# The first weight transfers of a linear-attention and MoE kernel, begun by GpSimd's DMA queue instead of SyncE's

## The chip, the cores and the metric

The kernel runs on one core of one Trainium2 chip. A core has TensorE (PE; its weight loads are listed as PEld), VectorE (DVE), ScalarE (ACT), GpSimd (POOL) and SyncE (SP), which work through queues of their own and meet by semaphores. Transfers run on 16 DMA engines and are begun by an instruction in the queue of SyncE, GpSimd or another engine. The metric is the device time of one execution in microseconds (us), the median of several runs.

## The reference

Three blocks follow each other. The first is a recurrence over 768 steps for 4 x 8 heads with a state of 40 x 40 each; the second and third are dense layers over its 3072 outputs of 320 numbers.

```python
for t in range(S):                      # B, H, S, D = 4, 8, 768, 40
    y[:, :, t] = einsum('bhd,bhde->bhe', rt, state)
    Sa = einsum('bhde,bhe->bhd', state, at)
    state = state * wt[:, :, None, :] - einsum('bhd,bhe->bhde', Sa, bt)
    state = state + einsum('bhd,bhe->bhde', vt, kt)
x = y.transpose(0, 2, 1, 3).reshape(3072, 320)
a, b = x @ w1, x @ w2                   # 320 x 1024 each
x = (a * b @ w3) @ w_out                # 1024 x 1024, 1024 x 320
h = maximum(x @ w_in, 0.0)              # 320 x 2048
return (h * h) @ w_out2                 # 2048 x 320
```

The weights come as 64-bit floats, the other inputs as 32-bit.

## The kernel before

**The scan.** The recurrence is cut into 24 chunks of 32 steps. What of a chunk doesn't depend on the state is prepared ahead (`prep`): its image `im` (k, b, a and the decay w, one transfer of 839 KB for the first chunks, in two pieces later) is loaded, VectorE makes running products of the decay (L553 `suf`, L563 `wi`), five multiplies scale the image (L575 with `wi`, L581 four times with `suf`; VectorE does them for chunks 0 to 3, GpSimd after that), TensorE multiplies the pieces (`prep_pq`, L594), ScalarE copies one half of the result (L598), VectorE transposes the other (L599 `qt`) and it is masked (L601, VectorE or GpSimd). `prep_kb` turns the scaled image (L611, ScalarE's copy L615). The results go to memory (`AW_d`, `Q_d`, `KB_d`) and are loaded again by the chunk that needs them. For four chunks at a time VectorE solves a triangular system (`solve`, from L646 to L665). It needs `pq` of all four.

**The chunk itself** is a chain through the state: `do_x0` (L739), `do_sa` (L749, copied by ScalarE to SA in L751), `do_sat` (L756, copies L758 and L761), `do_l` (L769, VectorE's L774), `do_z` and `do_ys` (L797, then VectorE's L805 and L809). `corner` (L687, L690, ScalarE's L694 and L698) finishes a piece of the first solve. Chunk c is computed while chunk c + 6 is prepared.

**The dense layers.** `w3` and `w_out` are multiplied into one matrix first (`fold`), and TensorE's gaps in the scan are filled with that and with the tiles of the second block (`a_tile`: L370 `ab`, L428 `px`) as the scan's outputs come. From 740 us on only the third block runs (L370 `ph`, L994 `po`).

**The weights.** `fetch` brings a piece of a weight matrix and decodes the 64-bit floats: a transfer (L319), two instructions of ScalarE (L325, L326) and two of VectorE (L328, L330). For `w1` and `w2` ScalarE and GpSimd then split it into two parts (L340 and L341, L353 and L354). `early` is true for `wo` (eight transfers of 320 KB), `w3t` (16 of 512 KB) and `w1` and `w2` (12 of 512 and 256 KB), and is set to false behind the scan's loop (L944), before `win` and `wo2`. The first pieces go into memory that is used later for other things (tile `early`), the rest through three buffers `raw` (`WB = (3, 4, 2)`), so such a transfer waits for the decode of the one three before.

**What sets the order.** TensorE's order is written by hand (`OPENING`, `BETWEEN`, the gaps `GAP0` and so on, and the queue `fill` of work that fills gaps). The other engines are ordered by a scheduler with priorities (`FIRST` for the chain, `SECOND` for `prep` and `solve`) that goes by estimates of when each instruction is ready. The loads and stores of `prep` go through `q_["prep"]`, which is SyncE's queue for chunks 0 to 9 and GpSimd's from chunk 10 on.

Of the kernel before, what the change touches and what calls it, by code (L numbers as in the profile page):

```python
# [243 lines left out]
def body(tc, img, rv, rd, vn, vp, raw, w1, w2, w3t, wo, win, wo2, ident, maskt, out, dbg=None):  # L244
    nc = tc.nc
    mm = nc.tensor.matmul
    act, dve, pool, sp = nc.scalar, nc.vector, nc.gpsimd, nc.sync

    with (
# [12 lines left out]
        with right, tc.manual_schedule(engines={mybir.EngineType.PE}):  # L262
# [8 lines left out]
            def staged(pl, tags, words):  # L271

                slots, n = staging.setdefault(tags, (deque(), [0]))
                if not slots:
                    t = pl.tile([128, 2048], U32, name="early", tag=tags[n[0] % len(tags)])
                    n[0] += 1
                    slots.extend(t[:, i:i + words] for i in range(0, 2049 - words, words))
                return slots.popleft()

            staging = {}  # L280
            early = True
# [13 lines left out]
            def fetch(pl, K, N, parts, dst=None, tag="fold"):  # L295

                place = None
                if early:
                    count[tag] += 1
                    if tag == "split" and count[tag] <= SPLIT_STAGED:  # L300
                        place = staged(ma, ("gh", "gl"), 1024)
                    elif tag == "fold" and not w12 and count[tag] <= FOLD_STAGED:
                        place = staged(wa, ("w1h", "w1l", "w2h"), 640)
                tag = "split" if early and tag == "split" else "wst"
                if dst is not None:
                    o = dst
                else:
                    o = pl.tile([128, K, N], F32, name="wst", tag=tag, bufs=bufs[tag])
                if not is64:
                    for p, f, src in parts:  # L310
                        sp.dma_start(out=o[p, f], in_=src)
                    return o
                if place is not None:
                    rt = place[:, 0:2 * K * N]
                else:
                    rt = pl.tile([128, 2 * K * N], U32, name="raw", tag="raw", bufs=bufs["raw"])
                rv_ = rt.rearrange("p (k n) -> p k n", k=K)
                for p, f, src in parts:
                    sp.dma_start(out=rv_[p, f], in_=src)  # L319
                w2_ = rt.rearrange("p (k n j) -> p k n j", k=K, j=2)  # L320
                hi, lo = w2_[:, :, :, 1], w2_[:, :, :, 0]
                ou = o.bitcast(U32)


                act.activation(out=o, in_=hi.bitcast(F32), func=AF.Copy, scale=2.0 ** -112)  # L325
                act.activation(out=lo, in_=lo, func=AF.Copy, scale=2.0 ** -29, bias=LOW)  # L326
                with tc.issue_after(hold[-1]) if hold else nullcontext():
                    dve.scalar_tensor_tensor(out=ou, in0=ou, scalar=3, in1=lo, op0=ALU.logical_shift_left,  # L328
                                             op1=ALU.bitwise_or)
                    dve.scalar_tensor_tensor(out=ou, in0=hi, scalar=0x80000000, in1=ou, op0=ALU.bitwise_and,  # L330
                                             op1=ALU.bitwise_or)
                return o

            def split_w(pl, src, h, l, j, k):

                n = 512 if early else 256

                t = fetch(pl, 1, n, [(slice(0, 128), 0, wcols(src, n * j, n)[128 * k:128 * k + 128])], tag="split")
                f = slice(n * j, n * j + n)
                act.copy(out=h[:, k, f], in_=t[:, 0])  # L340
                pool.tensor_tensor(out=l[:, k, f], in0=t[:, 0], in1=h[:, k, f], op=ALU.subtract)  # L341

            def split_r(pl, two):

                n = 512 if early else 256


                t = fetch(pl, 1, n, [(slice(64 * i, 64 * i + 64), 0, wcols(src, c, n)[256:320])
                                       for i, (src, c, _) in enumerate(two)], tag="split")
                for i, (_, c, r) in enumerate(two):  # L350
                    p, q = slice(64 * i, 64 * i + 64), slice(64 - 64 * i, 128 - 64 * i)
                    f = slice(c, c + n)
                    act.copy(out=r[p, f], in_=t[p, 0])  # L353
                    pool.tensor_tensor(out=r[q, f], in0=t[p, 0], in1=r[p, f], op=ALU.subtract)  # L354
# [88 lines left out]
            def fold(solved):  # L443
# [5 lines left out]
                def load_w3(i):  # L449
                    f, g = i // 2, i % 2  # L450
                    w3[i] = fetch(wf, 4, 128, [(slice(0, 128), slice(0, 4), wcols(w3t, 128 * f, 128)[
                        512 * g:512 * g + 512, :].rearrange("(k p) f -> p k f", p=128))])
# [39 lines left out]
            with (  # L492
# [381 lines left out]
                for c in range(NCH):  # L874
                    last = c == NCH - 1
                    p = c + 6
# [67 lines left out]
            early = False  # L944
# [189 lines left out]
```

## Time and profile before

| | us |
|---|---|
| median of three runs | 1076.19 |
| the three runs | 1075.29, 1082.97, 1076.19 |
| the profiled execution, its time | 1078.62 |
| the profiled execution, its span | 1076.7 |
| TensorE busy in the span | 917.4 (85%) |
| VectorE busy | 714.0 (66%) |
| ScalarE busy | 442.1 (41%) |
| GpSimd busy | 233.3 (22%) |

The span is the stretch from the first to the last instruction that the profiler recorded; the time of the execution is 1.9 us longer. Busy times of different engines overlap. Rows of a timeline give the start, the busy time, the engine (SPq is SyncE's queue of issues) and the line, then the operation, what it writes and from what, and how many such instructions are taken together. In square brackets stands how long the engine was idle just before, and what released it.

### The profile page before, as it was taken

How to read it: one execution, taken by the hardware profiler on the slowest of the kernel's cores; microseconds unless marked ns; L12 is line 12 of the kernel's file. 1: busy time of each engine (PE TensorE's matmuls, PEld its weight loads, DVE VectorE, ACT ScalarE, POOL GpSimd, SP SyncE). 2: the span in 40 equal slices, each digit the busy share in tenths (PEclk: the TensorE clock that was granted, in tenths of full speed). 3: DMA queues.
4: the chain of work that ended last, by engine and by line, in shares of the span. 5: the costliest groups of instructions: out<-in, count | busy, mean ns of one | idle time of the engine just before them, and what ended most of it. 6: DMA issues, size and time to landing. Idle time of an engine off the chain costs nothing.

```text
span 1076.7 us, 29204 instructions
## 1 busy us (share of the span) xinstructions
PE 917.4 (85%) x12240; PEld 823.3 (76%) x12240; DVE 714.0 (66%) x1399; ACT 442.1 (41%) x942; POOL 233.3 (22%) x304
## 2 busy tenths in 40 slices
PE   1327866689989898988999989879999999999997
PEld 1315544588888888887899879868989889898886
DVE  6864879958975996798589344897455554444432
ACT  2424555343434323433343333785433333333332
POOL 0261224433343343434200000562000000000000
PEclk9999988899999899989999999999999999999999
DMA  8976775666666567765744542666122221000001
GB/s 211 312 228 181 215 238 152 163 177 161 168 158 166 147 154 170 173 152 146 182 119 110 129 97 63 159 182 126 30 61 49 63 48 25 2 25 1 18 8 27
DMA packets 208922, 134.44 MB, mean 125 GB/s; under 512 B 143742, under 2 KB 184063, under 8 KB 208369
## 3 DMA queue, kind: packets, MB, share of 16 engines
q1 hardware_dynamic: 201424, 110.61, 40.3%
q0 software_dynamic: 7072, 21.57, 7.2%
q8 instruction: 98, 1.61, 0.7%
q10 hardware_dynamic: 288, 0.33, 0.1%
q14 instruction: 40, 0.32, 0.1%
HBM read 99.27 MB, written 33.19 MB: 123 GB/s over the span
## 4 chain that ended last, share of the span: by engine, by line
PE 52%; DVE 23%; DMA 12%; issue 4%; ACT 4%; SPq 2%; POOL 2%; ACTq 0%; DVEq 0%; POOLq 0%
PE ph L370 15%; PE po L994 15%; PE ab L370 9%; PE px L428 4%; DVE tmp L653 4%; DVE T L656 4%; PE pat L797 2%; DVE wst L328 2%; DVE yst L809 2%; DVE RX L805 2%; DMA im<-img 2%; DMA raw<-w3t 2%; PE pat L769 2%; DMA AW_d<-wi 2%; PE pat L782 1%
## 5 line engine op out<-in xcount | busy, mean ns | idle before, releaser
L994 PE MATMUL po<-wuh,rl 128*128 128x320 f32 x384 | 117.2, 308 | 1.7 <-DVE rl L981 1.7
L994 PE MATMUL po<-wul,rh 128*128 128x320 f32 x384 | 118.3, 308 | 0.0
L994 PE MATMUL po<-wuh,rh 128*128 128x320 f32 x384 | 118.0, 308 | 0.0
L370 PE MATMUL ab<-xh,w1h 128*128 128x256 f32 x192 | 60.0, 313 | 24.6 <-DVE g L402 23.8
L407 ACT CAST gh<-g 128x256 fp32r<-128x256 f32 x96 | 38.9, 405 | 99.2 <-DVE g L402 99.1
L370 PE MATMUL ph<-xh,wih 128*128 128x512 f32 x192 | 76.0, 396 | 2.8 <-issue 2.8
L370 PE MATMUL ph<-xh,wil 128*128 128x512 f32 x192 | 75.7, 394 | 0.0
L370 PE MATMUL ph<-xl,wih 128*128 128x512 f32 x192 | 75.6, 394 | 0.0
L994 PEld LDWEIGHTS po<-wul,rh 128*128 128x128 f32 x384 | 72.0, 188 | 4.3
L994 PEld LDWEIGHTS po<-wuh,rh 128*128 128x128 f32 x384 | 72.0, 188 | 3.8
L994 PEld LDWEIGHTS po<-wuh,rl 128*128 128x128 f32 x384 | 71.7, 188 | 2.4 <-DVE rl L981 2.2
L428 PE MATMUL px<-wph,gh 128*128 128x320 f32 x192 | 65.6, 342 | 2.7 <-ACT gh L407 2.7
L656 DVE TENSOR_TENSOR T<-T,tmp 128x31 f32<-128x31 f32 (+20 forms) x170 | 65.6, 386 | 3.0
L797 PE MATMUL pat<-YI,YR 128*40 128x72 f32 (+1 forms) x1536 | 57.4, 237 | 11.5 <-ACT kn L615 6.7
L653 DVE TENSOR_TENSOR tmp<-PT,T 128x31 f32<-128x31 f32 (+20 forms) x170 | 64.9, 382 | 3.5
L408 DVE TENSOR_TENSOR gl<-g,gh 128x256 fp32r<-128x256 f32 x96 | 45.1, 470 | 33.1 <-ACT gh L407 32.9
L581 POOL TENSOR_TENSOR im<-im,suf 104x256 f32<-104x256 f32 x80 | 65.6, 849 | 0.0
L797 PEld LDWEIGHTS pat<-YI,YR 128*40 128x40 f32 x1536 | 53.1, 125 | 16.1 <-ACT kn L615 7.3
L428 PE MATMUL px<-wph,gl 128*128 128x320 f32 x192 | 61.3, 319 | 0.8 <-DVE gl L408 0.7
L428 PE MATMUL px<-wpl,gh 128*128 128x320 f32 x192 | 60.9, 317 | 0.0
L370 PE MATMUL ph<-xq,wir 128*128 128x512 f32 x192 | 60.3, 394 | 0.0
L401 ACT COPY a_sb<-ab 128x256 f32<-128x256 f32 x96 | 35.6, 371 | 58.6 <-PE ab L370 58.1
(539 smaller groups left out, 2452.6 us busy)
## 6 DMA issues: line engine op xcount, KB each, us to landing
raw<-w3t SPq DMA_DIRECT2D x16, 512.0 KB
YR<-KB_d SPq DMA_DIRECT2D x48, 160.0 KB
im<-img POOLq DMA_DIRECT2D x28, 240.0 KB, 4.6
wt<-AW_d SPq DMA_DIRECT2D x24, 214.5 KB
raw<-wo SPq DMA_DIRECT2D x16, 320.0 KB
RX<-vp SPq DMA_DIRECT2D x24, 208.0 KB
vs<-rv SPq DMA_DIRECT2D x24, 208.0 KB
KB_d<-kn POOLq DMA_DIRECT2D x14, 320.0 KB, 5.6
```

The costliest lines, as they stand in the source:

```text
L328: dve.scalar_tensor_tensor(out=ou, in0=ou, scalar=3, in1=lo, op0=ALU.logical_shift_left, op1=ALU.bitwise_or)
L370: mm(out=ps, lhsT=seq[i][0], rhs=seq[i][1], start=(i == 0), stop=(i == 7))
L401: act.copy(out=a_sb, in_=ps[:, 0])
L407: act.copy(out=t["gh"][:, ff], in_=g)
L408: dve.tensor_tensor(out=t["gl"][:, ff], in0=g, in1=t["gh"][:, ff], op=ALU.subtract)
L428: mm(out=ps, lhsT=a_, rhs=b_, start=(k == 0 and i == 0), stop=(k == 7 and i == 2))
L581: eng.tensor_tensor(out=kb[:, g, :, :, j], in0=kb[:, g, :, :, j], in1=sg, op=ALU.mult)
L653: dve.tensor_tensor(out=tv, in0=Pv[:, :, s, s + 1:n].unsqueeze(3).to_broadcast(sh), in1=Tv[:, :, s, 0:s + 1].unsqueeze(2).to_broadcast(sh) ...
L656: return dve.tensor_tensor(out=o, in0=o, in1=tv, op=ALU.subtract).ins
L769: mm(out=ps[q:q + 64, 0, 32 * i - q // 2:32 * i - q // 2 + 64], lhsT=vs[0:104, i], rhs=RT[0:104, :, i], start=True, stop=True, tile_positi ...
L797: mm(out=ps[64 * y:64 * y + D, b, 72 * z:72 * z + n], lhsT=YR[:, u], rhs=YI[:, u, 0:n], start=True, stop=True, tile_position=(0, 64 * y))
L994: mm(out=po[j][g], lhsT=a_, rhs=b_, start=(ff == 0 and i == 0), stop=(ff == 15 and i == 2))
```

## The change

While `early` is true, the issue of a weight transfer is an instruction of GpSimd's queue. Nothing else is written differently; the scheduler then gives another order on the engines that it orders.

```diff
@@ -316,7 +316,7 @@
                     rt = pl.tile([128, 2 * K * N], U32, name="raw", tag="raw", bufs=bufs["raw"])
                 rv_ = rt.rearrange("p (k n) -> p k n", k=K)
                 for p, f, src in parts:
-                    sp.dma_start(out=rv_[p, f], in_=src)
+                    (pool if early else sp).dma_start(out=rv_[p, f], in_=src)
                 w2_ = rt.rearrange("p (k n j) -> p k n j", k=K, j=2)
                 hi, lo = w2_[:, :, :, 1], w2_[:, :, :, 0]
                 ou = o.bitcast(U32)
```

**The opening, GpSimd's queue.** The constants (`mark`, and `T`, the solve's matrix) are set here, then come the multiplies of chunk 4 (`im_105`, `wi_444`, `suf_440`). Before:

```order
8 L642 MEMSET T_338 128x1056
9 L840 MEMSET mark_93 128x17
10 L643 MEMSET T_338 128x32
11 L575 ISA
12 L575 TENSOR_TENSOR im_105<-im_105,wi_444 104x512
13 L581 TENSOR_TENSOR im_105<-im_105,suf_440 104x8x32 x4
```

And with the change:

```order
8 L642 MEMSET T_338 128x1056
9 L319 DMA early_519<-wo 128x640 x3
10 L319 DMA early_535<-wo 128x640 x3
11 L319 DMA early_551<-wo 128x640
12 L840 MEMSET mark_93 128x17
13 L319 DMA early_551<-wo 128x640
14 L643 MEMSET T_338 128x32
15 L319 DMA raw_563<-w3t 128x4x256
16 L319 DMA raw_570<-w3t 128x4x256
17 L319 DMA raw_577<-w3t 128x4x256
```

Seven issues of `wo` stand ahead of the last memset of `mark`, and the first three of `w3t` ahead of chunk 4's multiplies.

**The opening, VectorE.** `im_105`, `im_111` and `im_113` are the images of chunks 0, 1 and 2, with `suf_120`, `suf_133` and `suf_146`. Before:

```order
4 L553 SCALAR_TENSOR_TENSOR suf_120<-iw_106,mark_93 104x529
5 L559 SCALAR_TENSOR_TENSOR gc_95<-suf_120 104x16
6 L561 RECIPROCAL inv_94<-gc_95 104x16
7 L581 TENSOR_TENSOR im_105<-im_105,suf_120 104x8x32 x2
8 L563 SCALAR_TENSOR_TENSOR wi_124<-iw_106,inv_94 104x528
9 L581 TENSOR_TENSOR im_105<-im_105,suf_120 104x8x32 x2
10 L575 TENSOR_TENSOR im_105<-im_105,wi_124 104x512
11 L553 SCALAR_TENSOR_TENSOR suf_133<-im_111,mark_93 104x529
```

And with the change:

```order
4 L553 SCALAR_TENSOR_TENSOR suf_120<-iw_106,mark_93 104x529
5 L553 SCALAR_TENSOR_TENSOR suf_133<-im_111,mark_93 104x529
6 L559 SCALAR_TENSOR_TENSOR gc_95<-suf_120 104x16
7 L581 TENSOR_TENSOR im_105<-im_105,suf_120 104x8x32 x4
8 L559 SCALAR_TENSOR_TENSOR gc_95<-suf_133 104x16
9 L581 TENSOR_TENSOR im_111<-im_111,suf_133 104x8x32
10 L561 RECIPROCAL inv_94<-gc_95 104x16
11 L581 TENSOR_TENSOR im_111<-im_111,suf_133 104x8x32
12 L553 SCALAR_TENSOR_TENSOR suf_146<-im_113,mark_93 104x529
```

The scan of chunk 1 now stands ahead of chunk 0's multiplies, so all of chunk 0's work waits for chunk 1's image too; the scan of chunk 2 stands among the multiplies of chunk 1.

**The first solve, VectorE.** `T_338` is the solve's matrix; `suf_614` and `wi_618` belong to chunk 5, whose image is `im_612`, `qt_488` to chunk 4. Before, the stretch from the last steps of the solve on:

```order
75 L656 TENSOR_TENSOR T_338<-T_338,tmp_388 128x2x15
76 L328 SCALAR_TENSOR_TENSOR wo_sb_518<-wo_sb_518,early_519 128x320 x3
77 L659 STREAM_TRANSPOSE tt_339<-T_338 128x8x32 x2
78 L665 STREAM_TRANSPOSE early_103<-T_338 128x8x32 x2
79 L328 SCALAR_TENSOR_TENSOR wo_sb_518<-wo_sb_518,early_535 128x320 x2
80 L553 SCALAR_TENSOR_TENSOR suf_614<-im_612,mark_93 104x529
81 L866 COPY YI_506<-idt_63 40x32x40
```

And with the change, in the middle of the solve:

```order
61 L659 STREAM_TRANSPOSE tt_339<-T_338 128x8x32 x2
62 L553 SCALAR_TENSOR_TENSOR suf_614<-im_612,mark_93 104x529
63 L656 TENSOR_TENSOR T_338<-T_338,tmp_367 128x2x8x8
64 L559 SCALAR_TENSOR_TENSOR gc_95<-suf_614 104x16
65 L653 TENSOR_TENSOR tmp_370<-PT_337,T_338 128x126
66 L561 RECIPROCAL inv_94<-gc_95 104x16
67 L599 STREAM_TRANSPOSE qt_488<-pat_455 128x256
68 L656 TENSOR_TENSOR T_338<-T_338,tmp_370 128x2x7x9
69 L563 SCALAR_TENSOR_TENSOR wi_618<-im_612,inv_94 104x528
70 L866 COPY YI_506<-idt_63 40x32x40
```

Both scans of chunk 5 and the copy into YI moved from behind the solve to its middle.

**The same stretch, GpSimd.** The multiplies of chunk 5 (`im_612`) and of chunk 6 (`im_105`, `suf_629`, `wi_633`). Before:

```order
19 L581 TENSOR_TENSOR im_612<-im_612,suf_614 104x8x32 x4
20 L601 TENSOR_TENSOR qt_488<-qt_488,msk_64 128x256
21 L581 TENSOR_TENSOR im_105<-im_105,suf_629 104x8x32 x4
22 L575 TENSOR_TENSOR im_612<-im_612,wi_618 104x512
23 L575 TENSOR_TENSOR im_105<-im_105,wi_633 104x512
```

And with the change:

```order
26 L581 TENSOR_TENSOR im_612<-im_612,suf_614 104x8x32 x2
27 L601 TENSOR_TENSOR qt_488<-qt_488,msk_64 128x256
28 L575 TENSOR_TENSOR im_612<-im_612,wi_618 104x512
29 L581 TENSOR_TENSOR im_612<-im_612,suf_614 104x8x32 x2
30 L642 MEMSET T_1417 128x1056
31 L581 TENSOR_TENSOR im_105<-im_105,suf_629 104x8x32 x4
```

All of chunk 5 now stands ahead of chunk 6.

**The first chunks, ScalarE.** The place of the first copy of SA, among decodes of `w3t` (`raw_591`, `raw_1143`, `raw_1166`). Before:

```order
44 L326 ACTIVATE raw_584<-raw_584 128x512
45 L326 ACTIVATE raw_591<-raw_591 128x512
46 L326 ACTIVATE raw_1143<-raw_1143 128x512
47 L598 COPY Pn_104<-pat_755 128x2x4x32
48 L326 ACTIVATE raw_1166<-raw_1166 128x512
49 L751 COPY SA_102<-pat_793 128x8x40
```

And with the change:

```order
42 L598 COPY Pn_104<-pat_755 128x2x4x32
43 L751 COPY SA_102<-pat_793 128x8x40
44 L761 COPY YI_506<-SA_102 32x8x40 x4
45 L758 COPY vs_602<-pat_827 104x4x4x32
46 L325 ACTIVATE wst_583<-raw_584 128x512
47 L326 ACTIVATE raw_584<-raw_584 128x512
```

The copy of SA now comes ahead of these decodes.

**The first chunks, GpSimd.** The mask of chunk 7 (`qt_1398`) and the multiplies of chunk 8 (`wi_1528`, `suf_1524`). Before:

```order
29 L341 TENSOR_TENSOR w1l_1736<-wst_1759,w1h_1735 128x512
30 L601 TENSOR_TENSOR qt_1398<-qt_1398,msk_64 128x256
31 L575 TENSOR_TENSOR im_105<-im_105,wi_1528 104x512
32 L581 TENSOR_TENSOR im_105<-im_105,suf_1524 104x8x32 x4
33 L341 TENSOR_TENSOR w2l_1739<-wst_1750,w2h_1738 128x512
```

And with the change:

```order
49 L319 DMA raw_1350<-w3t 128x4x256
50 L319 DMA raw_1576<-w3t 128x4x256
51 L341 TENSOR_TENSOR w1l_1736<-wst_1759,w1h_1735 128x512
52 L601 TENSOR_TENSOR qt_1398<-qt_1398,msk_64 128x256
53 L319 DMA raw_1628<-w3t 128x4x256
54 L319 DMA early_2099<-w2 128x1024
55 L319 DMA early_2099<-w1 128x1024
56 L575 TENSOR_TENSOR im_105<-im_105,wi_1528 104x512
57 L581 TENSOR_TENSOR im_105<-im_105,suf_1524 104x8x32 x4
```

Issues of `w3t`, `w1` and `w2` stand ahead of the mask and of the multiplies.

## Rows read from the trace of the kernel before

**Rows 1.** The page: TensorE's and the other engines' busy time; the chain that ended last.

```profile
PE 917.4 (85%) x12240; PEld 823.3 (76%) x12240; DVE 714.0 (66%) x1399; ACT 442.1 (41%) x942; POOL 233.3 (22%) x304
...
PE 52%; DVE 23%; DMA 12%; issue 4%; ACT 4%; SPq 2%; POOL 2%; ACTq 0%; DVEq 0%; POOLq 0%
```

**Rows 2.** Windows by stage: stretch, length, busy time of each engine, clock, DMA share, GB/s.

```profile
0.00:35.40 35.40, 6.29 (x264) 5.13 (x264) 24.68 (x47) 13.88 (x28) 2.35 (x9) 1.00 0.89 250
35.40:89.60 54.20, 18.16 (x580) 15.23 (x580) 40.94 (x85) 16.95 (x38) 27.29 (x22) 1.00 0.75 229
89.60:194.90 105.30, 76.31 (x1404) 55.74 (x1404) 81.38 (x145) 53.98 (x110) 32.77 (x33) 0.87 0.72 198
194.90:740.00 545.10, 487.51 (x8176) 450.89 (x8170) 409.04 (x897) 234.67 (x565) 169.52 (x240) 0.95 0.60 150
740.00:1076.70 336.70, 329.08 (x1825) 296.34 (x1823) 157.93 (x228) 122.60 (x205) 1.36 (x1) 0.99 0.13 31
```

**Rows 3.** A window of the opening, the same columns.

```profile
4.00:12.00 8.00, 0.91 (x64) 0.91 (x64) 4.88 (x9) 0.88 (x1) 0.00 (x0) 1.00 0.99 222
```

**Rows 4.** Timeline of VectorE, opening and first solve.

```profile
4.36 1.26 DVE L553 TENSOR_TENSOR_SCAN suf<-iw,mark 104x529 f32<-104x529 f32 x1 [1.03 <-DMA iw<-img]
...
12.68 1.26 DVE L553 TENSOR_TENSOR_SCAN suf<-im,mark 104x529 f32<-104x529 f32 x1 [1.64 <-DMA im<-img]
...
22.54 1.26 DVE L553 TENSOR_TENSOR_SCAN suf<-im,mark 104x529 f32<-104x529 f32 x1 [1.98 <-DMA im<-img]
...
35.36 2.13 DVE L646 STREAM_TRANSPOSE PT<-early 128x256 f32<-128x256 f32 x4 [2.25 <-ACT early L598]
...
53.54 1.25 DVE L553 TENSOR_TENSOR_SCAN suf<-im,mark 104x529 f32<-104x529 f32 x1
54.71 1.52 DVE L866 COPY YI<-idt 40x1280 f32<-40x1280 f32 x1
...
68.34 1.24 DVE L563 TENSOR_TENSOR_SCAN wi<-im,inv 104x528 f32<-104x528 f32 x1
```

**Rows 5.** Timeline of SyncE's queue, the transfers of wo.

```profile
4.39 4.27 SPq L319 DMA_DIRECT2D early<-wo  x3
...
23.16 3.31 SPq L319 DMA_DIRECT2D early<-wo  x5
```

**Rows 6.** Timeline of TensorE, chunks 0 to 2.

```profile
73.17 1.18 PE L594 MATMUL pat<-im 40*32 40x64 f32 x64 [10.24 <-POOL im L575]
...
83.63 1.10 PE L756 MATMUL pat<-idt,SA 128*104 128x128 f32 x4 [8.06 <-ACT SA L751]
...
124.35 0.86 PE L594 MATMUL pat<-im 40*32 40x64 f32 x64
...
143.28 1.10 PE L756 MATMUL pat<-idt,SA 128*104 128x128 f32 x4 [8.65 <-ACT SA L751]
```

**Rows 7.** Timeline of ScalarE, ahead of two copies of SA.

```profile
82.60 0.67 ACT L326 ACTIVATE raw<-raw 128x512 uint32<-128x512 uint32 x1 [2.12 <-DMA raw<-w3t]
...
140.29 0.62 ACT L357 CAST xh<-xf 128x512 fp32r<-128x512 f32 x1 [3.85 <-DMA xf<-X_d]
```

**Rows 8.** Waits of SyncE's queue, 0 to 200 us: total, times, longest.

```profile
SPq L319 <- DVE wst L330: 17.9, 7, 4.1
```

**Rows 9.** Timeline of GpSimd, two issues for other transfers.

```profile
219.12 1.05 POOL L548 DMA_DIRECT2D iw<-img  x2 [2.91 <-DVE wi L563]
...
233.47 0.56 POOL L616 DMA_DIRECT2D KB_d<-kn  x1
```

**Rows 10.** Timeline of GpSimd, multiplies of chunks 5 to 7.

```profile
57.39 8.75 POOL L581 TENSOR_TENSOR im<-im,suf 104x256 f32<-104x256 f32 x4
...
68.34 3.65 POOL L581 TENSOR_TENSOR im<-im,suf 104x256 f32<-104x256 f32 x4
71.94 1.17 POOL L575 TENSOR_TENSOR im<-im,wi 104x512 f32<-104x512 f32 x1
...
107.76 2.63 POOL L581 TENSOR_TENSOR im<-im,suf 104x256 f32<-104x256 f32 x4
```

## The prediction

> **What bounds the kernel now.** First the page: TensorE is busy for 85% of the span and VectorE for 66%, and the chain that ended last runs 52% over TensorE, 23% over VectorE and 12% over transfers [rows 1]. One bound for the whole span would mislead, so I read the time by stage next [rows 2]. After 740 us TensorE is busy for 329 of 337 us, and from 195 to 740 us for 488 of 545. Before 195 us it isn't the bound: 101 us of 195, and in the first 90 only 24. All 36 transfers that the change touches are begun before 178 us (the 36 issues of L319 that the SyncE timeline shows up to there), so what the change can do to the time it does in those first 195 us. There VectorE is busy for 24.7 of 35.4 us, then 40.9 of 54.2, then 81.4 of 105.3 [rows 2]; its idle time in the second and third stage, 13.3 and 23.9 us, limits what any earlier transfer can give while VectorE's work stays the same.
>
> Then who waits for whom. In the opening the 16 DMA engines are full: from 4 to 12 us they are busy for 99% and move 222 GB/s [rows 3]. VectorE gets the fourth image at 22.54 us and starts the first solve at 35.36 [rows 4]. SyncE begins three transfers of `wo` at 4.39 us, behind the images, and the other five at 23.16 [rows 5]. Later TensorE waits 10.24 us for GpSimd's multiply before `pq` of chunk 5 at 73.17, 8.06 us for ScalarE's copy of SA at 83.63, and 8.65 us for the next but one such copy at 143.28 [rows 6]. What held ScalarE is in its timeline: at 82.60 it decodes a piece of `w3t` for which it had waited 2.12 us, with the copy of SA next in its queue; up to 140.29 it waits 3.85 us for `xf`, whose transfer SyncE issued among the weights, and the copy of SA is behind that [rows 7]. SyncE stood 17.9 us, in seven waits, at a fetch whose buffer VectorE was still decoding, the longest 4.1 us, with every later load behind it [rows 8].
>
> **The change, part by part.** It moves 36 issues from SyncE's queue to GpSimd's. The bytes are the same and PE's order is written by hand and stays, but the orders of GpSimd, ScalarE and VectorE move with it (the three pieces above).
>
> (1) GpSimd's time. An issue there takes 0.525 us for 40 runs of memory (1.05 for two) and 0.56 for 128 [rows 9]. A piece of `w3t` has 512 runs, and no row shows such a one. If the price per run holds (0.035 us for 88 runs), it is 0.56 + 384 x 0.0004 = 0.71 us; if all of it goes by runs, 2.24. I take 0.71, the line through both rows: 16 x 0.71 + 20 x 0.56 = 23 us of GpSimd, at most 47. GpSimd is busy for 62 of the 195 us [rows 2], so this has room if it isn't in front of something urgent. In the opening eight issues of `wo`, 4.5 us, stand ahead of the last memset of `mark`, on which VectorE's first scan waits; seven of them end the memset at 2.62 + 7 x 0.56 = 6.5 us instead of 2.75. The scan ran at 4.36 [rows 4], but in the new order it is followed by the scan of chunk 1, whose image came for 12.68 [rows 4]; about 2 us of delay there lie under that wait. Without that cover they would cost 2.
>
> (2) Start to the first solve. All eight `wo` (2.6 MB) and three `w3t` (1.5 MB) now run beside the images, which came through full engines at 222 GB/s [rows 3]. The bytes of `wo` that were begun before image 3 arrived were three of eight; the five others, 1.6 MB, take 7 us at 222 GB/s, and if the engines share them evenly over the stretch, half, 3.5 us, falls on the image: it lands at 26 instead of 22.5. If all of them and `w3t` go ahead, 13 us later. On top, VectorE's new order scans chunk 1, 2 and 3 as early as it can and leaves multiplies for later: from the last image to the solve it did 12.8 us before [rows 4]; the new rows up to the solve (four more multiplies, two reciprocals, one scan, one transpose) sum to some 16 with the durations of the same lines, of which I count 2 as new, the others having been waited for. ScalarE's copies for the solve stand behind eight `wo` decodes in the new order, but these have landed by then. Loss: 3.5 + 2 = 5.6 us with rounding of the rows, from 2 to 13.
>
> (3) First solve to the first `do_ys` (35.36 to 89.64, 54.3 us). The scan of chunk 5 stood behind the solve at 53.54 and its second half at 68.34; now both stand inside the solve. So GpSimd can finish chunk 5 before it begins chunk 6. Before, it did four of chunk 5's five multiplies from 57.39 on, then a mask of 2.27 us and four of chunk 6 (3.65 us from 68.34), and the fifth of chunk 5, which TensorE waited for, only at 71.94 [rows 10]. The 10.24 us before 73.17 shrink by the 5.9 us of the mask and of chunk 6, and the 8.06 us before SA go, since in the new order the copy of SA stands ahead of the `w3t` decodes. That is 14 us. Against it, the solve is longer by chunk 5's work (1.25 + 1.25 + 1.5 for the scans and the copy into YI [rows 4], half a microsecond of small ones), 4.5 us, which is taken out behind the solve but lies on its chain now; two thirds of it come back because VectorE then has no such work at 66 us. What is late next is `qt`, the transpose on VectorE that follows `pq` of chunk 5. Gain 14 - 3 = 11 us; at most the 18 of both waits and 2 beside them, at worst a loss of 2 if the solve carries all and the wait is merely renamed.
>
> (4) First `do_ys` to 195 us (105 us, VectorE 81.4). The 8.65 us before the copy of SA of chunk 2 go, as ScalarE's split of `xf` now stands behind it. The 17.9 us of SyncE's stalls move to GpSimd's queue; behind them there stand the multiplies of chunks 7 to 9. Chunk 7's set started at 107.76 and took 2.63 us [rows 10], and its `pq` ran at 124.35 [rows 6]: 14 us of slack against a longest wait of 4.1. The loads of the scan's inputs (XL, RT, YI) no longer stand behind a blocked fetch. I count 8.65 less 3.6 for work of VectorE that then is late next: 5 us gained, from 16 (two thirds of VectorE's idle 23.9) to a loss of 8 (half of the 17.9 lands on the path).
>
> (5) After 195 us: nothing. The fetches of `win` and `wo2` stay on SyncE, and TensorE is 90% busy or more.
>
> Sum: +5.6 - 11 - 5 = -10.4 us on the profiled execution's 1078.62 us, so 1068.2. That execution is 2.4 us above the median of 1076.19 of the runs shown, so 1065.8, and I say 1066.
>
> What no row here shows is a fetch of weights through GpSimd's queue. Other transfers do go through it from 219 us on, at half a microsecond each [rows 9]. The Trainium skill, "DMA: Bandwidth & Descriptors", under "Issuing engine by pattern", says that transfers whose descriptors hardware makes, as for SyncE, are generally faster than those that GpSimd writes, and gives about 1 us to the first byte against 0.6. On the 13 fetches of `w3t` that wait for a buffer, an estimate by that page, this would be 5 us more, and the sum about 1071.
>
> **Rivals.** *Nothing is won (A).* The transfers end on the same 16 engines, and the stalls were SyncE's, not the path's: VectorE's work sets the length of both later stages, so the removed waits come back at `qt` and the decodes. For it speak VectorE's 77% share in stage three; against it that TensorE's three waits of 27 us name other engines. Half of the gains, 8 us, against 5.6 lost: 1074. The Trainium skill states this one as a rule, in "DMA: Bandwidth & Descriptors", section "Issuing engines are not separate DMA queues": starting transfers on other engines saves only the issuing time; [rows 8] bear on it, since what SyncE lost there was waiting, which the rule leaves out.
>
> *Slower (B).* GpSimd's queue is in order, and it computes as well as issues. In the new order each late `w3t` fetch waits for the decode of the one three before, which waits for VectorE; behind it stand the multiplies and the `qt` mask of the next chunk, for which `pq` and thus TensorE wait. If VectorE's decodes fall behind, all 17.9 us [rows 8] become GpSimd's and, past the slack of 14 us per chunk summed over chunks, TensorE's. It decides once a wait at such a fetch is longer than about 14 us instead of 4.1. Then +5.6 - 11 + 17.9 = +12.5: 1091 on the profiled execution, 1089 on the median.
>
> *More is won (C).* With the stalls off SyncE all loads come early and VectorE fills its idle time: 13.3 us in stage two and 16 of 23.9 in stage three, less 5.6: -23.7, or 1052.5.
>
> **How the numbers follow.** The forecast (4 to 16 us gained, 1060 to 1072) gets 0.50, A 0.18, B 0.20, C 0.12. One per cent, 10.8 us, is about what a measurement of this kernel tells from no change (the three runs shown lie within 0.7%). Faster by over 1%, under 1065.4: all of C and half of the forecast, 0.12 + 0.24 = 0.36. Slower, over 1087: three quarters of B, 0.15. The rest, 0.49, is within 1%. The range runs from 1054, which leaves the lower half of C out, to 1087, which leaves most of B out.
>
> **What would show it.** Right: the solve starts near 41 us; `pq` of chunk 5 waits for GpSimd under 5 us; ScalarE's copy of SA isn't preceded by a decode; the first `do_ys` comes near 84 and the first `ab` near 185. Wrong: image 3 lands after 30 us (term 2); GpSimd's queue shows waits at L319 for VectorE of over 10 us with L575 or L601 behind (B); GpSimd's issues of `w3t` take over 1 us (term 1); or the time before 195 us is shorter while the rest is longer by as much.

## The result, and the profile after

The change made the kernel slower: 1086.72 us against 1075.74 (medians of 20 runs each), a ratio of 1.0085 with a 95% interval of 1.0062 to 1.0109. (The ratio compares the fast runs of both kernels alone; the quotient of the two medians is 1.0102.) That is on the other side of the forecast. It lies inside the range that I gave, 1054 to 1087, by 0.3 us, and that is luck: the forecast itself ended at 1072, and what lay above was room for rivals A and B, whose mechanisms aren't what happened. The profiled execution of the changed kernel took 1088.52 us with a span of 1086.7. The rows that answer to [rows 1] and [rows 2]:

```profile
PE 918.0 (84%) x12240; PEld 822.5 (76%) x12240; DVE 713.0 (66%) x1399; ACT 442.3 (41%) x942; POOL 258.5 (24%) x340
...
PE 52%; DVE 20%; DMA 14%; issue 5%; ACT 4%; SPq 4%; POOL 1%; ACTq 0%; POOLq 0%; DVEq 0%
```

```profile
0.00:35.40 35.40, 3.48 (x124) 2.99 (x128) 18.76 (x38) 12.57 (x23) 8.96 (x20) 1.00 0.90 234
35.40:89.60 54.20, 20.54 (x677) 16.70 (x661) 40.53 (x87) 15.78 (x37) 32.02 (x27) 1.00 0.73 213
89.60:194.90 105.30, 78.60 (x1476) 56.93 (x1477) 83.61 (x150) 55.78 (x113) 43.89 (x51) 0.89 0.79 212
194.90:740.00 545.10, 478.93 (x8122) 443.13 (x8121) 403.17 (x886) 229.40 (x554) 167.91 (x238) 0.95 0.58 147
740.00:1086.70 346.70, 336.44 (x1866) 302.73 (x1864) 166.94 (x242) 128.79 (x219) 5.67 (x5) 0.99 0.15 35
```

Busy times of TensorE, VectorE and ScalarE are the same within 1 us; GpSimd has 25 us more, 23 of them for the 36 issues. Up to 194.9 us TensorE did 102.6 us of work against 100.8, so the time isn't lost there as a whole. A finer table tells it, by the start of the same instructions in both traces (first solve: L646; x0: L739, ys: L797, by chunk, counted from 0):

| | before | after | difference |
|---|---|---|---|
| first solve | 35.36 | 43.62 | +8.3 |
| ys of chunk 0 | 89.64 | 93.48 | +3.8 |
| ys of chunk 2 | 168.96 | 169.13 | +0.2 |
| x0 of chunk 4 | 206.40 | 206.60 | +0.2 |
| ys of chunk 4 | 233.32 | 243.63 | +10.3 |
| ys of chunk 8 | 328.47 | 339.01 | +10.5 |
| ys of chunk 23 | 671.61 | 681.45 | +9.8 |
| end of the span | 1076.7 | 1086.7 | +10.0 |

What the opening loses has been made up by chunk 2, and then one chunk takes 10 us longer, once.

**The opening.** VectorE's timeline (as in [rows 4]): the images of chunks 1 and 3 are scanned at 14.22 and 27.93 us instead of 12.68 and 22.54, and the first solve, begun at 43.62, ends at 67 instead of 49.8.

```profile
14.22 1.26 DVE L553 TENSOR_TENSOR_SCAN suf<-im,mark 104x529 f32<-104x529 f32 x1 [6.29 <-DMA im<-img]
...
27.93 1.26 DVE L553 TENSOR_TENSOR_SCAN suf<-im,mark 104x529 f32<-104x529 f32 x1 [2.22 <-DMA im<-img]
...
43.62 2.13 DVE L646 STREAM_TRANSPOSE PT<-early 128x256 f32<-128x256 f32 x4 [1.33 <-ACT early L598]
...
66.89 0.19 DVE L656 TENSOR_TENSOR T<-T,tmp 128x30 f32<-128x30 f32 x1
```

GpSimd's timeline (as in [rows 9, 10]) and its waits at fetches from 0 to 200 us (as in [rows 8]: total, times, longest):

```profile
2.63 3.88 POOL L319 DMA_DIRECT2D early<-wo  x7
...
14.22 0.76 POOL L319 DMA_DIRECT2D raw<-w3t  x1 [6.98 <-DMA early<-wo]
...
71.95 11.65 POOL L581 TENSOR_TENSOR im<-im,suf 104x256 f32<-104x256 f32 x4 [0.77 <-DMA im<-img]
...
83.60 2.31 POOL L319 DMA_DIRECT2D raw<-w3t  x3
```

```profile
POOL raw L319 <- DVE wst L330: 5.0, 2, 2.9
...
POOL raw L319 <- DVE gc L559: 4.6, 1, 4.6
```

Issues of `wo` take 0.55 us each, one of `w3t` 0.76. The four multiplies of chunk 6 take 11.65 us beside VectorE's decodes, where such a set took 2.6 to 8.8 before [rows 10], and three fetches of `w3t` stand behind them. Their decode then stands in ScalarE's queue ahead of a copy of `corner` (L694), and TensorE waits 5.94 us for that copy:

```profile
88.18 0.66 ACT L325 ACTIVATE wst<-raw 128x512 f32<-128x512 f32 x1 [9.79 <-DMA raw<-w3t]
...
89.28 0.26 ACT L694 ACTIVATE x<-pat 128x128 f32<-128x128 f32 x1
```

```profile
69.39 1.05 PE L687 MATMUL pat<-tt,early 32*32 32x16 f32 x64 [9.06 <-DVE tt L659]
...
75.96 1.09 PE L756 MATMUL pat<-idt,SA 128*104 128x128 f32 x4 [0.55 <-ACT SA L751]
80.70 1.05 PE L687 MATMUL pat<-tt,early 32*32 32x16 f32 x64 [3.65 <-DVE qt L599]
...
89.60 0.73 PE L690 MATMUL pat<-x,early 32*16 32x16 f32 x64 [5.94 <-ACT x L694]
93.48 3.61 PE L797 MATMUL pat<-YI,YR 128*40 128x72 f32 x64 [3.15 <-issue]
```

So the wait of 8.06 us before chunk 0's `do_sat` [rows 6] is 0.55 us now, and three new ones, 3.65, 5.94 and 3.15 us, have come behind it. The wait of 10.24 us for GpSimd's multiply [rows 6] has gone too, but TensorE now waits 9.06 us for the end of the solve (L659) instead: chunk 0's L749 begins at 74.12 us, and it began at 74.28 before.

**Chunk 4.** TensorE's timeline before, and then after:

```profile
206.40 0.27 PE L739 MATMUL pat<-RX,XL 128*32 128x40 f32 x4 [1.59 <-issue]
...
215.10 1.29 PE L749 MATMUL pat<-X,tt 32*32 32x40 f32 x64 [1.58 <-DVE tt L659]
...
219.60 0.60 PE L756 MATMUL pat<-idt,SA 128*104 128x128 f32 x4
...
223.01 1.15 PE L769 MATMUL pat<-RT,vs 104*64 104x64 f32 x32 [1.85 <-ACT vs L758]
...
233.32 2.20 PE L797 MATMUL pat<-YI,YR 128*40 128x72 f32 x64
```

```profile
206.60 0.27 PE L739 MATMUL pat<-RX,XL 128*32 128x40 f32 x4 [1.71 <-issue]
...
219.03 1.29 PE L749 MATMUL pat<-X,tt 32*32 32x40 f32 x64 [6.05 <-DVE tt L659]
...
226.84 1.10 PE L756 MATMUL pat<-idt,SA 128*104 128x128 f32 x4 [3.33 <-ACT SA L751]
...
231.80 1.15 PE L769 MATMUL pat<-RT,vs 104*64 104x64 f32 x32 [2.15 <-ACT vs L758]
...
243.63 2.20 PE L797 MATMUL pat<-YI,YR 128*40 128x72 f32 x64
```

The solve of chunks 4 to 7 ends later (6.05 us of waiting for `tt`, 3.9 us lost), and then TensorE waits for ScalarE's copies of SA and of vs. Against the kernel before, L749 is 3.9 us late, L756 7.2, L769 8.8 and ys 10.3. The last 1.5 us of these come from the granted clock. The windows below (columns as in [rows 2]), before and after, hold the same 49 matmuls from L769 on, and behind the two waits TensorE runs most of them at the lower of its two levels, 1.2 GHz (mean 0.64 of full speed instead of 1.00):

```profile
223.00:226.20 3.20, 3.19 (x49) 2.99 (x49) 1.97 (x4) 1.17 (x3) 0.00 (x0) 1.00 0.73 194
```

```profile
231.80:236.50 4.70, 4.70 (x49) 4.44 (x49) 2.50 (x5) 1.44 (x4) 0.00 (x0) 0.64 0.42 80
```

ScalarE's timeline there, before and after:

```profile
206.72 0.49 ACT L325 ACTIVATE wst<-raw 128x320 f32<-128x320 f32 x1 [4.74 <-DMA raw<-wo]
...
216.59 0.42 ACT L751 COPY SA<-pat 128x320 f32<-128x320 f32 x1
...
222.39 0.57 ACT L758 COPY vs<-pat 104x512 f32<-104x512 f32 x1
```

```profile
219.27 0.43 ACT L325 ACTIVATE wst<-raw 128x256 f32<-128x256 f32 x1 [4.88 <-DMA raw<-win]
...
225.73 0.43 ACT L325 ACTIVATE wst<-raw 128x256 f32<-128x256 f32 x1 [5.71 <-DMA raw<-win]
...
226.38 0.41 ACT L751 COPY SA<-pat 128x320 f32<-128x320 f32 x1
...
231.18 0.57 ACT L758 COPY vs<-pat 104x512 f32<-104x512 f32 x1
```

Before, ScalarE had done the first three pieces of `win` and was at the first of `wo2` by 206.72 us, and it copied SA 1.5 us after L749 had begun. Now it waits 4.88 and 5.71 us for pieces of `win`, with the copy of SA behind. SyncE's queue, before and after, says why they are late:

```profile
195.94 2.21 SPq L319 DMA_DIRECT2D raw<-win  x4
```

```profile
208.65 0.35 SPq L319 DMA_DIRECT2D raw<-win  x1
...
214.44 1.46 SPq L319 DMA_DIRECT2D raw<-win  x2
...
219.72 0.60 SPq L319 DMA_DIRECT2D raw<-win  x1
```

`win` was begun at 195.94 us; now the first piece at 208.65, behind the loads of YR and YI, the others at 214.44 and 219.72, behind more loads. The last split of `w2`, on GpSimd, starts at 203.23 us instead of 194.58 (before, `win` was begun as soon as that split ended, at 195.9), and the scheduler had put the issue further back.

### The profile page after: what moved, and what is told of

The parts are those of the page before. It is cut to its first block, busy times and chain, and to the rows that moved or that the text cites. A ratio compares the mean times of both kernels' runs of the same rounds, so it can differ in the third digit from the quotient of the medians.

```text
span 1086.7 us, 29239 instructions
## 1 busy us (share of the span) xinstructions
PE 918.0 (84%) x12240; PEld 822.5 (76%) x12240; DVE 713.0 (66%) x1399; ACT 442.3 (41%) x942; POOL 258.5 (24%) x340
## 4 chain that ended last, share of the span: by engine, by line
PE 52%; DVE 20%; DMA 14%; issue 5%; ACT 4%; SPq 4%; POOL 1%; ACTq 0%; POOLq 0%; DVEq 0%
PE ph L370 15%; PE po L994 15%; PE ab L370 9%; DVE T L656 3%; DVE tmp L653 3%; PE px L428 3%; PE pat L797 3%; DMA raw<-w3t 2%; DMA X_d<-yst 2%; DVE RX L805 2%; DMA xr<-X_d 2%; DMA KB_d<-kn 2%; DVE yst L809 2%; DMA im<-img 2%; DMA early<-wo 2%
## 5 line engine op out<-in xcount | busy, mean ns | idle before, releaser
L581 POOL TENSOR_TENSOR im<-im,suf 104x256 f32<-104x256 f32 x80 | 69.9, 901 | 0.8 <-DMA im<-img 0.8
L797 PE MATMUL pat<-YI,YR 128*40 128x72 f32 (+1 forms) x1536 | 56.0, 234 | 9.3 <-DVE qt L599 4.8
L797 PEld LDWEIGHTS pat<-YI,YR 128*40 128x40 f32 x1536 | 51.6, 123 | 14.4 <-DVE qt L599 6.0
L402 DVE TENSOR_TENSOR g<-a_sb,ab 128x256 f32<-128x256 f32 x96 | 39.9, 416 | 32.5 <-ACT a_sb L401 31.3
```

The source lines that it names most:

```text
L402: dve.tensor_tensor(out=g, in0=a_sb, in1=ps[:, 1], op=ALU.mult)
L581: eng.tensor_tensor(out=kb[:, g, :, :, j], in0=kb[:, g, :, :, j], in1=sg, op=ALU.mult)
L797: mm(out=ps[64 * y:64 * y + D, b, 72 * z:72 * z + n], lhsT=YR[:, u], rhs=YI[:, u, 0:n], start=True, stop=True, tile_position=(0, 64 * y))
```

## The experiments

Each kernel ran in five rounds against the kernel before on the same chip. The table has for every kernel the time that chunk 4 took in its trace, from x0 (L739) to ys (L797):

| kernel | ratio | interval | chunk 4, us |
|---|---|---|---|
| before | 1 | | 26.9 |
| changed | 1.0085 | 1.0062 to 1.0109 | 37.0 |
| changed, again (e12) | 1.0113 | 1.0069 to 1.0156 | 37.1 |
| e1, wo alone | 1.0007 | 0.9983 to 1.0032 | 24.7 |
| e2, w3t alone | 0.9991 | 0.9966 to 1.0017 | 28.6 |
| e3, w1 and w2 alone | 0.9943 | 0.9914 to 0.9971 | 24.6 |
| e3 again (e14) | 0.9973 | 0.9941 to 1.0004 | 24.4 |
| e4, all but wo | 1.0076 | 1.0044 to 1.0108 | 24.8 |
| e5, changed + edge | 0.9984 | 0.9960 to 1.0008 | 27.9 |
| e7, e4 + edge | 1.0072 | 1.0036 to 1.0107 | 23.3 |
| e8, e3 + edge | 0.9959 | 0.9928 to 0.9989 | 26.3 |
| e9, before + edge | 0.9981 | 0.9954 to 1.0008 | 24.5 |
| e6, before, win late | 0.9968 | 0.9935 to 1.0001 | 22.8 |
| e10, before, win late, decodes ahead | 1.0008 | 0.9981 to 1.0036 | 29.5 |
| e11, e10 with the third piece later | 1.0061 | 1.0034 to 1.0087 | 36.9 |
| e13, changed, win begun by GpSimd | 1.0102 | 1.0068 to 1.0137 | 38.7 |

The theory (T1): the loss is made at chunk 4, by ScalarE's queue, where the copies of SA and vs stand behind decodes of `win` that wait for their transfers. Rivals: GpSimd's queue is blocked at fetches with multiplies behind (T2); the opening's 8 us (T3).

**e5, the decodes behind the copies.** In `do_sat` the copy of vs is remembered, `marks["vs", c] = act.copy(...)`, and ScalarE's part of the first step of eight is queued behind it:

```diff
             for j in range(8):
-                for k in range(2):
-                    split_w(wst, win, wih, wil, j, k)
+                with tc.issue_after(marks["vs", 4].ins) if j == 0 else nullcontext():
+                    for k in range(2):
+                        split_w(wst, win, wih, wil, j, k)
...
```

> The changed kernel, with one edge more: on ScalarE the decodes of the first pieces of win and wo2 stand behind chunk 4's copy of vs (L758), where they stood ahead of its copy of SA. Theory T1: the change's loss is made at the change-over. The changed kernel is level with the one before up to chunk 4's x0 (206.6 against 206.4 us) and 10.3 us behind at chunk 4's ys; of that 3.9 us are there before the copy of SA (the second solve ends late) and the rest comes from ScalarE, which waits for late win pieces with the copies of SA and vs behind them. T1 expects chunk 4's ys about 6 us earlier than in the changed kernel (near 237.5 us), the ratio to the kernel before at 1.003 to 1.004. Rival T2: the loss is GpSimd's blocked queue and its multiplies, wherever it shows; then the ratio stays at 1.008.

0.9984: the whole loss is gone, more than the two thirds that I expected. ScalarE's timeline of e5:

```profile
220.76 0.42 ACT L751 COPY SA<-pat 128x320 f32<-128x320 f32 x1 [5.27 <-PE pat L749]
...
225.31 0.59 ACT L758 COPY vs<-pat 104x512 f32<-104x512 f32 x1 [0.48 <-PE pat L756]
225.92 0.43 ACT L325 ACTIVATE wst<-raw 128x256 f32<-128x256 f32 x1
```

The copy of SA comes 1.35 us after L749 at 219.41, the decodes behind the copy of vs. `win` is as late as before this edit (first piece 211.14 us) and costs nothing now. L749 is as late as in the changed kernel (219.41 us against 219.03), so that delay alone doesn't make the loss. All 36 fetches are still begun by GpSimd, so T2 falls for this loss.

**e1, e2, e3: one matrix at a time.** The condition at the issue, with `dst` set for `wo` alone and `tag` "split" for `w1` and `w2`:

```diff
-                    (pool if early else sp).dma_start(out=rv_[p, f], in_=src)
+                    (pool if early and dst is not None else sp).dma_start(...)              # e1
+                    (pool if early and dst is None and tag == "wst" else sp).dma_start(...) # e2
+                    (pool if early and tag == "split" else sp).dma_start(...)               # e3
```

> Only the eight transfers of wo are begun by GpSimd, those of w3t, w1 and w2 by SyncE as before. T1: the opening loses some 8 us (first solve begins near 43 us instead of 35), which is gone by chunk 2's ys, since that stood at 169 us in both kernels; the change-over is as before, so the ratio is 0.998 to 1.003. Rival T3, that the opening's 8 us are what is lost in the end: 1.007 to 1.009.

> Only the 16 transfers of w3t are begun by GpSimd. T1: what delays the change-over is that GpSimd's last splits of w1 and w2 (L354) come late, 204.5 us against 195.9, and that SyncE waits with chunk 9's Q_d ahead of win; w3t alone does part of that by its issues and waits ahead of the splits, and I expect a ratio of 1.002 to 1.006. T2, which puts the loss on GpSimd's waits at fetches of w3t: 1.008. T3 (opening): 1.000, since these three early pieces come behind the images.

> Only the 12 transfers of w1 and w2 are begun by GpSimd. T1: these are the last that GpSimd must begin and split before win can start, so the change-over may come late as well: 1.000 to 1.006, and if the first win fetch is issued later than 203 us, above 1.003. T2 and T3: 0.998 to 1.002, since no wait of w3t and nothing of the opening is moved.

e1 starts its first solve at 46.45 us, 11 us late, later than the changed kernel, and is not slower than the kernel before: T3 falls. e2 is level, below what T1 and T2 expected. e3 is faster by 0.6%, which no theory had. So none of the three parts has the loss alone.

**e9 and e6: the edge alone, late win alone.** e9 is e5 with `sp.dma_start`. e6 is the kernel before with `tc.issue_after(marks["yr", 4].ins)` around the same block, where `marks["yr", c]` is SyncE's second load of YR for chunk c (so for chunk 4, not 5 as the text below has it).

> The kernel before, with the edge of e5 alone: ScalarE's decodes of the first win and wo2 pieces stand behind chunk 4's copy of vs; all fetches begun by SyncE. A control. T1: in the kernel before the first win pieces are begun at 195.9 us and wait little, so the edge gives back little: ratio 0.997 to 1.002, chunk 4's ys at 231 to 234 us (233.3 before). If the edge were a gain of its own, so that e5 proves nothing on the change, it would give 0.990 to 0.992 here.

> The kernel before, with the first transfers of win and wo2 put behind SyncE's second load of YR for chunk 5's inputs, where they stood in the changed kernel (208.65 us against 195.94). T1 in its narrow form, that a late start of win is enough: ratio 1.004 to 1.008. If it needs ScalarE's order as well (here the scheduler leaves one decode of win ahead of chunk 4's copy of SA, in the changed kernel three): 1.000 to 1.003.

The edge gives 0.2% to the kernel before, within its interval, and 1% to the changed one (1.0085 to 0.9984). Late `win` with one decode ahead costs nothing (0.9968): the narrow form of T1 falls.

**e4 and e7: wo left on SyncE.** The condition is `early and dst is None`, in e7 with the edge of e5.

> The changed kernel with wo left on SyncE: w3t, w1 and w2 are begun by GpSimd. The opening is then as before (first solve near 36 us). T3 (the opening is what is lost): 0.995 to 1.000. T1: it depends on where the scheduler puts the decodes of win; with the order of the changed kernel (three ahead of chunk 4's copy of SA) 1.003 to 1.008, else 0.992 to 0.998.

> w3t, w1 and w2 begun by GpSimd, wo by SyncE, and the edge of e5. T1: opening and change-over both as before, and the gain that e2 and e3 showed apart (0.9991 and 0.9943) stays: 0.990 to 0.996. If the two queues of GpSimd's fetches disturb each other (T2): 0.998 to 1.003.

Both lose 0.7 to 0.8%, with the edge or without, and chunk 4 is quick in both (24.8 and 23.3 us): a second, different loss, and the traces don't show where it is made. By x0 of chunk 3 both are late, at 183.0 and 183.5 us against 176.75; but e1 stands at 182.3 there, is later than both at ys of chunk 4 (239.0 us against 237.9 and 236.9), and isn't slower. VectorE's and GpSimd's timelines of e4 show about half of the lateness at chunk 3:

```profile
175.26 5.88 DVE L328 SCALAR_TENSOR_TENSOR wst<-wst,raw 128x512 uint32<-128x512 uint32 x1
181.06 0.98 DVE L805 TENSOR_TENSOR RX<-pat,gc 40x320 f32<-40x320 f32 x2
```

```profile
175.61 1.19 POOL L575 TENSOR_TENSOR im<-im,wi 104x512 f32<-104x512 f32 x1
176.76 2.60 POOL L581 TENSOR_TENSOR im<-im,suf 104x256 f32<-104x256 f32 x4
179.32 1.26 POOL L341 TENSOR_TENSOR w1l<-wst,w1h 128x512 fp32r<-128x512 f32 x1
```

One decode, 0.68 us elsewhere, takes 5.88 us and ends half a microsecond behind GpSimd's row of six instructions (L575, L581 four times, L341); the RX that TensorE waits for (L805) is behind it. In e7 it is 5.87 us at the same place. GpSimd also stood 13.7 us ahead of two fetches of `w1` and `w2` in e4, 14.3 in e7, with a mask of `qt` behind them, the order of rival B; but in e4 that mask came at 97.88 us, and in the kernel before at 97.81, so the wait held nothing up there. No run took either of them away. Why e4 and e7 lose stays open.

**e10 and e11: the loss made in the kernel before.** All fetches by SyncE. The first piece of `win` is put behind YR, the second behind RX of chunk 5, and ScalarE's copy of SA behind the third decode; the first step also has the chain's priority, `FIRST`. e11 differs from e10 in one place:

```diff
-                    with tc.issue_after(marks["rx", 5].ins) if j == 0 else nullcontext():
+                    with tc.issue_after(marks["xr", 1].ins) if j == 0 else nullcontext():
                         if j < 4:
                             split_r(wst, [(win, 256 * j + 1024 * i, wir) for i in range(2)])
...
+                    tc.add_manual_dep(marks["sa", 4].ins, late[-3].ins.name, ...)  # both: SA behind the third decode
```

> The kernel before, all fetches begun by SyncE, with both things that the changed kernel showed at the change-over: the first transfers of win and wo2 as late in SyncE's queue as there (the first behind the second load of YR for chunk 4, the others behind the load of RX for chunk 5), and ScalarE's copy of SA of chunk 4 behind the decodes of the first three. With the kernel before (early, ahead), e9 (early, behind) and e6 (late, one ahead) this is the fourth of four. T1 in its wide form, that only both together cost: chunk 4's ys at 239 to 244 us and a ratio of 1.005 to 1.010. If the loss comes from elsewhere in the change: 0.997 to 1.002.

> As e10 (kernel before, first win pieces late, three decodes ahead of chunk 4's copy of SA), with the third piece behind SyncE's loads for the second tile of the dense layer, where its second half stood in the changed kernel; in e10 it landed at 217 us, in the changed kernel at 225.7. T1: the copy of SA then waits until 223 to 226 us instead of 218, chunk 4's ys at 239 to 242 us, and the ratio is 1.004 to 1.009. If a wait at this place is made up later: 0.998 to 1.003 although ys stands at 239 or later.

e10 missed: the third piece was decoded at 217.39 us and SA copied at 218.05, so there was little to wait for. In e11 ScalarE's timeline is that of the changed kernel:

```profile
224.71 0.43 ACT L325 ACTIVATE wst<-raw 128x256 f32<-128x256 f32 x1 [4.66 <-DMA raw<-win]
...
225.37 0.41 ACT L751 COPY SA<-pat 128x320 f32<-128x320 f32 x1
```

ys of chunk 4 comes at 243.83 us (changed kernel: 243.63), and the kernel is 0.6% slower with no fetch on GpSimd (the intervals of e10 and e11 just touch). That is most of the changed kernel's 0.85%. The loss rests on the times here, not on the trace: the traced execution of e11 took 1076.71 us, the second shortest of its twelve (median 1080.66), and by chunk 23's ys it had made up the 10.5 us (669.72 against 671.61), which the changed kernel's trace keeps (681.45). What gave them back isn't known.

**e13 and e12: win begun by GpSimd, and a second trace.** e13 sends the first step's transfers of `win` and `wo2` to GpSimd too; e12 is the changed kernel itself.

> The changed kernel, with the first transfers of win and wo2 (those of the first of eight steps) begun by GpSimd as well, behind its last split of w2. ScalarE's order is the one of the changed kernel: three decodes of win ahead of chunk 4's copy of SA. Only the start changes: near 205 us, all together, where SyncE began them from 208.65 to 221 us with other loads between. T1 (the copies of SA and vs wait for late win pieces): the third piece is there by 214 us, the copy of SA comes near 220 instead of 226.4, chunk 4's ys at 235 to 238 us, ratio 0.997 to 1.003. If lateness of win is not what costs: 1.006 to 1.010.

> The changed kernel once more, for a second trace on the chip of the two others and the spread of its times. Ratio 1.006 to 1.011; chunk 4's x0 at 204 to 210 us and its ys 36 to 38 us later, against 27 in the kernel before. If the second trace shows chunk 4 in 30 us or less and the loss elsewhere, T1 rests on one odd execution.

e12 shows the same step, x0 at 205.93 and ys at 243.05 us. e13 missed: GpSimd began `win` at 211.74 us, behind its other work, and not at 205. The third piece was there by 220.5 and SA copied at 221.17, but a later piece took its place, between the copy of SA and those into YI and vs:

```profile
221.17 0.42 ACT L751 COPY SA<-pat 128x320 f32<-128x320 f32 x1
229.52 0.43 ACT L326 ACTIVATE raw<-raw 128x256 uint32<-128x256 uint32 x1 [7.92 <-DMA raw<-win]
...
233.54 0.58 ACT L758 COPY vs<-pat 104x512 f32<-104x512 f32 x1
```

7.92 us of waiting there, vs at 233.54 us, and the ratio 1.0102. The piece waited for belongs to the second step, whose transfers SyncE still began, at 226.72 us. By this trace the mechanism is T1's, one copy further on; the remedy was none. So the kernels in which chunk 4 takes about 37 us or more (changed, e11, e13) lose 0.6 to 1.1%, and of the others only e4 and e7 lose.

**e8 and e14: the part that gains.** e8 is e3 with the edge, e14 is e3 once more.

> Only the 12 transfers of w1 and w2 begun by GpSimd (as e3, 0.9943) with the edge of e5. If the edge guards against late win pieces at no cost: 0.990 to 0.996. If e3's gain came from the order that the scheduler happened to find, it can go: 0.997 to 1.002.

> The kernel of e3 once more (only w1 and w2 begun by GpSimd), since it was the fastest of thirteen and the fastest of many is partly luck. If its gain is real: 0.992 to 0.998. If it was the spread of the runs: 0.998 to 1.002.

0.9959 and 0.9973. `w1` and `w2` alone on GpSimd give 0.3 to 0.6%, though the second measurement alone isn't clear of its interval, and the edge adds nothing. This is the fastest version found, and the fastest of many is partly luck; why it is faster stays open, since its two traces stand 1.0 and 2.8 us ahead at chunk 8's ys (327.47 and 325.70), about as much as repeated traces of one kernel differ (changed kernel: 339.01 and 336.84).

## Why the prediction was wrong

I forecast 1066 us and the median is 1086.7. By the spans of the two traces the change cost 10.0 us where the sum has 10.4 gained. Half of that miss is term (5), which I had written off in a line; the other half is terms (2) to (4), 6.6 us of it in (3).

- **(5) "After 195 us: nothing."** This failed first: +10.3 us in chunk 4. It rested on the step that since all 36 transfers are begun before 178 us, the change can act on the first 195 us only, and on `win` and `wo2` staying on SyncE. They do stay, but where they stand in its queue moved, and so did ScalarE's order around them: the copies of SA and vs stood behind decodes that waited 4.88 and 5.71 us for `win`. e5 (loss gone when the decodes stand behind the copies) and e11 (0.6% lost in the kernel before, by place and order alone) show it. The order of both kernels was there to be compared at chunk 4; I compared it only where the change's own fetches stand.
- **(3) First solve to first ys, 11 us gained.** 49.9 us instead of 54.3: 4.4 gained. Both waits that I counted went, but not their time. In place of the 10.24 us for GpSimd's multiply TensorE waits 9.06 us for the solve, which took 23.3 us instead of 14.3, twice the lengthening that I counted: this is the renamed wait that I had only as the worst case. (Besides chunk 5's work, VectorE stood 1.93 us in the solve, up to a store of `qt`, and 1.52 us for chunk 5's image.) The 8.06 us became 0.55, and "what is late next" was `qt` for 3.65 us and then ScalarE's copy of `corner` behind a `w3t` decode for 5.94.
- **(2) The opening, 5.6 us lost.** 8.3 lost, within my 2 to 13. The image landed 5.4 us later, not 3.5, and VectorE took 2.9 us more from there to the solve, where I had 2. e1 shows that such a loss need not reach the end.
- **(4) 5 us gained.** 3.6 us (from 93.48 to 206.60, 113.1 us, against 116.8). Right in size, and in the wait named: none is left before chunk 2's L756, at 142.31 us.
- **(1) 0.71 us for an issue of w3t.** 0.76 measured, 0.55 for one of `wo`. Right; GpSimd is busy 25 us longer, where I had 23.
- The sum of (2) to (4) by 206 us: +0.2 instead of -10.4.
- Slips of arithmetic: (3) takes off 3 where a third of 4.5 is 1.5; in (2), 3.1 MB at 222 GB/s are 14 us and not 13; in (4), half of 17.9 is 9 and not 8. None decides the outcome.
- **Rival B** came nearest in its time (1089) but not in its mechanism: the longest wait at a fetch that VectorE ended was 4.6 us (the profile puts it down to L559, which follows the decode), far from 14, and it was ScalarE's queue that blocked, not GpSimd's. In the opening GpSimd's own multiplies delayed fetches, the other way round.
- **The 0.36 for a gain over 1%** found no support: of the kernels with part of the change the best gives 0.3 to 0.6%.

The Trainium skill, "DMA: Bandwidth & Descriptors", section "Issuing engine by pattern", calls transfers of SyncE generally faster than GpSimd's. An issue of `w3t` took 0.76 us on GpSimd; e2, which moves all 16, is level (0.9991), so no run here shows a price on the path.

## What to carry to other kernels

A change of queue is also a change of order on every engine that a scheduler arranges: compare the orders over the whole stretch in which a moved instruction's followers run, the next user of its buffers above all, not only where the moved instructions stand. Look in each in-order queue for an instruction that waits for a transfer with a copy of the critical chain behind it: late transfers cost nothing until such a copy stands behind them (e6 and e11), and one order edge can take the cost away (e5). When parts of a change are measured one at a time, their sum says little: 0.9991 and 0.9943 made 1.0076 together.

## What the runs showed of the hardware

A VectorE instruction and GpSimd's were held up beside each other for far longer than one instruction: a decode with two inputs in SBUF took 5.88 us instead of 0.68 beside a row of six GpSimd instructions in e4, and four multiplies of GpSimd took 11.65 us beside VectorE's decodes in the changed kernel, against 2.6 at the least before. The Trainium skill, "SBUF — State Buffer", section "Who interferes with whom", says that a VectorE instruction with two SBUF inputs and a GpSimd instruction that reads SBUF contend for a shared port, and calls this contention an exclusive lock. The rows agree with it, in that each was slow beside the other; the wait in e4 lasted through several instructions of GpSimd that followed each other.

The runs of one kernel spread by 1.5% (1070.14 to 1086.30 us for the kernel before). Of this the end makes little: from chunk 23's ys on, all 16 traces took 403.7 to 405.5 us, and the two traces of the changed kernel, 4.2 us apart in their spans, differ by 0.9 there. A single trace's total is no measure of an edit below 1%.
